# Attention feeding a two-layer network on one core: float64 weights prepared in pairs, with g in pairs of chunks and another issue order

## The chip, the cores and the metric

One core of a Trainium2 chip runs the whole kernel. The metric is the device time of one execution in microseconds (us): for the kernel before, the median of three runs.

## What is computed

The input is q, k, v of shape (8 batches, 8 heads, 576 positions, 64) and f of shape (8, 8, 576), all float32, and two float64 weight matrices of 512 x 2048 and 2048 x 512. Cut to what matters:

```python
scores = q @ k.T / 8;  cum = cumsum(log(clip(f, 1e-4, 1)))
scores = where(causal, -1e9, scores + cum[:, None] - cum[None, :])
attn = softmax(scores);  x = (attn @ v) laid out as (4608 tokens, 512)
h = x @ w_in;  g = h * cos(h);  out = g @ w_out
```

## The kernel before, in words

**Tiling.** The work is 32 pairs of heads (8 batches of 4 pairs) and 16 units of the network (each batch in a unit of 320 tokens and one of 256). A pair's scores come in five row blocks for each of two heads; VectorE masks them and takes the row bound (lines 705, 879), ScalarE takes the exp (715, 884), and the weights of the attention go to f16 high and low parts (901, 905) or, for the first four pairs, stay in float32 (`attention32`). Their product with v, scaled and split into f16 parts xh and xl, is the input of the first layer.

A unit's first layer (`gemm1`, line 964) is four chunks of 512 hidden columns, each four groups of 12 matmuls. A chunk's h is evicted (970), and g = h cos h is made by VectorE and ScalarE (979 to 985) and split into a high and a low f16 part (992, 993 or 994). The second layer (`gemm2`, line 1010) is four blocks of output rows; each reads all four chunks of g, 48 matmuls. So TensorE runs 3072 dense matmuls in either layer.

**The weights.** Each matrix is cut into 16 pieces of 128 rows x 512 columns of 8-byte words, 512 KB. `stage` loads a piece into a raw tile (line 493) and rebuilds float32 from the two halves of each word in three VectorE operations (483, 487, 491) straight into the place of the next piece of W1s or W2s; `bound` squares it on ScalarE with a sum per row (502), as a bound of its size. When all pieces of a group are bounded, the scale follows, and `split` makes the f16 high and low parts in place (512, 519). W1's raw tiles are in the ring "h" (three tiles of 5 KB per partition), which the network's h uses later; W2's are in the ring "g" (eight tiles of 5 KB), which the chunks of g use later. A raw tile is free once its `bound` has run, since that writes its last 256 words as scratch.

**The order.** Every operation is numbered as the program makes it. `ORDER` (line 52) is a list, written out by hand, of all the numbers: `Plan.order` checks it against the dependencies and the ring sizes, and the operations are issued in it (line 1075). Each engine and SyncE's queue run their own operations in this order, each as soon as what it needs is there. A number with "a" runs its alternative on GpSimd (or VectorE). A number with "+n" has n filler matmuls ahead of it:

```python
for pads, fill, fn in seq:
    for _ in range(pads):
        T.matmul(fill(), ones, mask[:, 0:PAD], start=True, stop=True)   # line 1077
    fn()
```

A filler has 448 columns and its result is overwritten. All loads and stores but four go through SyncE's queue, in order; a transfer that waits holds up those behind it. The four are the cumulative rows of the first pair, which ScalarE issues (line 640).

**The opening.** f is loaded (451), clipped (452), its logarithm taken (453) and summed by a scan (455). Rows of that sum go into the tile Q beside q and k (load32: q and k at line 636, the rows at 640); with them the first scores of pair 0 can run (line 697 is the matmul of the pairs 0 to 3, 865 that of pairs 4 to 7, 867 and 868 that of the rest). The probabilities are transposed (668) and evicted (656), multiplied with v (742), and the result transposed again (765). `prep_vscale` loads v once more for a bound of its size (582, 584).

Of the kernel before, what the change touches and what calls it, by code (L numbers as in the profile page):

```python
# [23 lines left out]
P = 128  # L24
# [13 lines left out]
RAWS = {1: "h", 2: "g"}  # L38
CH = {1: 1, 2: 2}
# [9 lines left out]
BUFS = dict(xs=1, stage=2, v2=2, vv=2, pt3=3, pt2=2, xh0=8, xl0=8, xh1=8, xl1=8, h=3, r=1, g=8, ot=1,  # L49
# [11 lines left out]
260 325 544 294 296 545a 238 261 305 256 226 447 314 287a 546 263+1 257 8 326 262 242 239 264a 265 445 393 240 547 319 335 362 266+1 230 297  # L61
288 268 320 298 109 241 322 114 221 301 315 394 302 267 327 321 303 329 227 381 299 548 395 358 549 306 333 289 386 328 359 334 307 345 371
# [259 lines left out]
def fox_moe_kernel(ctx: ExitStack, tc: tile.TileContext, qkT, vp, fT, w1, w2, out):  # L322
# [142 lines left out]

    raws = {}

    def stage(w, k, src, pr):

        n = 1024 if wide else 512  # L470
        rb = ring("raw", [P, n + 256], I32, tag=RAWS[w])
# [4 lines left out]
        def wf():  # L476
            return wide_of(w, k)
# [472 lines left out]
    def gemm1(u, c, pr):  # L950
# [38 lines left out]
        def gx(i):  # L989
            return g.get()[:, i, :, 0:w_]  # L990
# [117 lines left out]
```

## Time and profile before

| | |
|---|---|
| three runs | 1041.29 us median, 1040.98 to 1046.04 |
| profiled execution | 1040.97 us, its span 1039.0 us |
| TensorE matmul, busy | 1027.0 us (99%) |
| TensorE weight loads, busy | 831.6 us (80%) |
| ScalarE, busy | 789.5 us (76%) |
| VectorE, busy | 774.9 us (75%) |
| GpSimd, busy | 294.8 us (28%) |
| DMA | 144.77 MB, mean 139 GB/s |

A row of a group of instructions gives the line, the engine, the operation, what it writes and reads by the program's names, the shape, the count, then the busy time in us and the mean of one in ns, and last the idle time of that engine just before them with what ended it. PE is TensorE's matmuls, PEld its weight loads, DVE VectorE, ACT ScalarE, POOL GpSimd, SP SyncE; SPq is an issue on SyncE's queue. Ends of matmuls are modelled and matmuls overlap, so their starts say more than their durations. The span is the profiled execution's time from the first to the last instruction; the execution's own time is 2 us longer.

### The profile page before, as it was taken

To read this page: it belongs to the slowest core of one execution; us is meant where nothing else is said; L and a number is where in the kernel's file an instruction comes from. 1 tells how busy PE (TensorE), PEld (TensorE's weight loads), DVE (VectorE), ACT (ScalarE), POOL (GpSimd) and SP (SyncE) were. 2 spreads that over 40 slices of the span, in tenths; PEclk is the share of its full clock that TensorE was granted. 3 is DMA by queue.
4 is the path that set the end of the run, shared out by engine and by line. 5 is a ranking of instruction groups with operands and counts; after the bars stand their busy time and mean duration, and the time that the engine had idled before them with its cause. 6 is when DMAs were issued, how large, how long until landed. Compare 5 with 4: busy or idle time off the path is not lost. (4 is left out here: it accounts for less than half of the span.)

```text
span 1039.0 us, 23384 instructions
## 1 busy us (share of the span) xinstructions
PE 1027.0 (99%) x8915; PEld 831.6 (80%) x8916; DVE 774.9 (75%) x1710; ACT 789.5 (76%) x1711; POOL 294.8 (28%) x381
## 2 busy tenths in 40 slices
PE   8999999999999999999999999999999999999998
PEld 4788777778888877888778877888778877888787
DVE  8999998778678676787877688586877967663531
ACT  5999999788768797898877789686878877753431
POOL 3223213432341343332332424233141313300110
PEclk9999999999999999999999999999999999999999
DMA  8997525856685757668465766947466583520001
GB/s 261 288 321 200 130 55 128 185 107 162 154 175 147 163 132 163 139 144 183 114 145 135 176 142 159 193 83 164 124 170 136 121 189 56 122 39 16 7 14 34
DMA packets 255920, 144.77 MB, mean 139 GB/s; under 512 B 223736, under 2 KB 231928, under 8 KB 255808
## 3 DMA queue, kind: packets, MB, share of 16 engines
q1 hardware_dynamic: 255680, 143.27, 58.4%
q8 instruction: 70, 1.15, 0.4%
q14 instruction: 42, 0.34, 0.1%
q10 hardware_dynamic: 128, 0.01, 0.0%
HBM read 71.41 MB, written 9.68 MB: 78 GB/s over the span
## 5 line engine op out<-in xcount | busy, mean ns | idle before, releaser
L1010 PE MATMUL hp<-g,W2s 128*128 128x320 f16 (+1 forms) x3072 | 391.8, 286 | 0.2
L964 PE MATMUL hp<-xh,W1s 128*128 128x320 f16 (+1 forms) x2048 | 381.3, 286 | 1.5 <-ACT h L970 1.4
L964 PEld LDWEIGHTS <-W1s 128*128 128x128 f16 x3072 | 295.5, 98 | 78.6 <-issue 1.8
L1010 PEld LDWEIGHTS <-W2s 128*128 128x128 f16 x3072 | 296.3, 98 | 76.1 <-issue 0.6
L964 PE MATMUL hp<-xl,W1s 128*128 128x256 f16 (+1 forms) x1024 | 292.6, 286 | 0.0
L905 DVE SCALAR_TENSOR_TENSOR PS<-pa,ri,PS 128x576 f16<-128x576 f32 (+3 forms) x280 | 146.1, 544 | 57.3 <-ACT PS L901 55.9
L884 ACT ACTIVATE pa<-pa,nb 128x576 f32<-128x576 f32 (+4 forms) x280 | 141.5, 506 | 48.5 <-DVE nb L879 43.1
L901 ACT ACTIVATE PS<-pa,ri 128x576 f16<-128x576 f32 (+3 forms) x280 | 137.7, 531 | 31.1 <-DVE ri L892 27.0
L889 POOL TENSOR_SCALAR ri<-L 128x1 f32<-128x1 f32 (+1 forms) x168 | 53.9, 321 | 352.0 <-ACT pa L884 347.1
L879 DVE CUSTOM_DVE_ANT_0 pa<-pa,mask 128x576 f32<-128x576 f32 (+4 forms) x280 | 134.7, 500 | 24.0 <-PE pa L868 20.4
L970 ACT ACTIVATE h<-hp 128x320 f32<-128x320 f32 (+1 forms) x256 | 100.1, 411 | 36.5 <-PE hp L964 32.8
L994 POOL TENSOR_TENSOR g<-h,g 128x1024 f16<-128x1024 f32 (+1 forms) x32 | 83.5, 2609 | 149.0 <-ACT g L992 147.3
L985 DVE TENSOR_TENSOR h<-h,r 128x1280 f32<-128x1280 f32 (+1 forms) x64 | 89.6, 1399 | 34.4 <-ACT r L983 33.9
L983 ACT ACTIVATE r<-r,halfpi,m_inv 128x1280 f32<-128x1280 f32 (+1 forms) x64 | 86.2, 1348 | 31.2 <-DVE r L981 29.0
L981 DVE SCALAR_TENSOR_TENSOR r<-r,m_b,h 128x1280 f32<-128x1280 int32 (+1 forms) x64 | 93.6, 1462 | 1.1
L867 PE MATMUL pa<-Q 128*128 128x288 f32 (+4 forms) x288 | 90.4, 327 | 1.2 <-DVE PS L905 0.7
L979 DVE TENSOR_SCALAR r<-h,m_a 128x1280 int32<-128x1280 f32 (+1 forms) x64 | 54.9, 858 | 44.9 <-ACT h L970 43.0
L992 ACT CAST g<-h 128x1280 f16<-128x1280 f32 (+1 forms) x64 | 73.8, 1154 | 10.6 <-DVE h L985 10.4
L934 PEld LDWEIGHTS <-vv 128*64 128x64 f16 x1512 | 68.6, 110 | 10.3 <-issue 9.5
L868 PE MATMUL pa<-Q 68*128 68x288 f32 (+4 forms) x288 | 76.6, 304 | 0.0
L934 PE MATMUL pa<-pt,vv 128*64 128x256 f16 (+2 forms) x1512 | 76.6, 254 | 0.0
L1016 ACT ACTIVATE ot<-hp,m_o 128x320 f32<-128x320 f32 (+1 forms) x64 | 32.2, 503 | 47.6 <-PE hp L1010 36.2
(127 smaller groups left out, 1182.5 us busy)
## 6 DMA issues: line engine op xcount, KB each, us to landing
stage<-in_dram SPq DMA_DIRECT2D x48, 576.0 KB
stage<-in_dram SPq DMA_DIRECT2D x32, 320.0 KB
v<-in_dram SPq DMA_DIRECT2D x32, 320.0 KB
h<-in_dram SPq DMA_DIRECT2D x16, 512.0 KB
g<-in_dram SPq DMA_DIRECT2D x16, 512.0 KB
Q<-Q SPq DMA_DIRECT2D x48, 144.0 KB
out_dram<-ot SPq DMA_DIRECT2D x32, 160.0 KB
Q<-in_dram SPq DMA_DIRECT2D x16, 288.0 KB
```

Source lines behind the costliest of these rows:

```text
L867: T.matmul(c, hi[:, 0, isl], hi[:, 1, d], start=True, stop=False)
L879: op("DVE", c_dve(w) + 0.008, lambda view=view, ib=ib, o=o, w=w, mk=mk, c=c: V.tensor_tensor_reduce(out=view(ib, o, w), in0=view(ib, o, w) ...
L884: op("ACT", c_act(w, True, 2), lambda view=view, ib=ib, o=o, w=w, c=c: A.activation(view(ib, o, w), view(ib, o, w), AF.Exp, bias=nb.get()[ ...
L901: op("ACT", c_act(w, True, 1), lambda view=view, ib=ib, o=o, w=w, c=c, out_=out_: A.activation(out_(0), view(ib, o, w), AF.Copy, scale=ri. ...
L905: op("DVE", c_dve(w) + 0.06, lambda view=view, ib=ib, o=o, w=w, c=c, out_=out_: V.scalar_tensor_tensor(out_(1), view(ib, o, w), ri.get()[: ...
L934: T.matmul(d, vv.get()[:, jb, hd, kv], m, start=first and x == 0, stop=last and x == 2)
L964: T.matmul(hp.get()[:, 0:w_], WS_[1][:, at(1, 4 * c + cb), w, fs], x.get(), start=(n == 0), stop=(n == 11))
L970: op("ACT", c_act(w_, True), lambda hp=hp, k=k: A.activation(h.get()[:, k, 0:w_], hp.get()[:, 0:w_], AF.Copy, scale=float(2.0 ** -24)), re ...
L981: op("DVE", c_dve(N) + 0.045, lambda: V.scalar_tensor_tensor(fl(r), fl(r).bitcast(I32), b1.get()[:, c:c + 1], fl(h), op0=ALU.mult, op1=ALU ...
L983: op("ACT", c_act(N, aps=2), lambda: A.activation(fl(r), fl(r), AF.Sin, scale=inv.get()[:, c:c + 1], bias=halfpi), reads=[inv], writes=[r] ...
L985: op("DVE", c_dve(N), lambda: V.tensor_tensor(fl(h), fl(h), fl(r), op=ALU.mult), reads=[r], writes=hk, prio=pr)
L1010: T.matmul(po.get()[:, 0:w_], WS_[2][:, at(2, 4 * c + k), w, msl], gh.get()[:, i, k, 0:w_], start=(n == 0), stop=(n == 47))
```

## The change

**Pairs.** `stage` and `bound` get a count m of pieces. The first four pieces of W1 (one group) stay single; the other twelve of W1 and all sixteen of W2 are loaded, converted and bounded two at a time, with 1024 words per partition and instruction: 18 loads instead of 32, 54 conversions on VectorE instead of 96, 18 bounds on ScalarE instead of 32. A pair is two rows of 4 KB per partition in the source, as two pieces were. The maxima run over half as many columns. `split` stays as it is.

**Rings.** Raw tiles of pairs, of W1 and W2 alike, are in the ring "g", now four tiles of 10 KB; single ones are in "h". The temporary `chl` of `decay` goes from "g" to "h". Two chunks of g share a tile of 10 KB, so that the ring still holds the g of two units.

**Order.** The program makes 4229 operations instead of 4299, and `ORDER` is another list throughout. Of the 821 groups of matmuls none is added or left out. The fillers:

- before: 99 in 32 places, 44 of them ahead of the first scores (`33+44`). 88 stand ahead of the first group of the first dense layer, and 11 between that and the first group of the second layer.
- after: 119 in 41 places, 52 of them ahead of the first scores (`33+52`). 104 stand ahead of the first group of the first dense layer, 13 between that and the first group of the second layer, 2 later.

The opening of SyncE's queue, by what is moved:

- before: f; W1 pieces 0, 2, 1; Q of pair 0, second head, then first head; W1 piece 3 (waits for the bound of piece 0); v of pair 1 for its bound; a row of pair 1 (waits for the scan); W2 pieces 0 and 1; a row; W1 pieces 4, 5; ...
- after: v of pair 1 for its bound; f; W1 pieces 0, 1, 2; two rows of pair 1 (wait for the scan); Q of pair 0, first head; two rows of pair 1; W1 piece 3 (waits for the bound of piece 0); Q of pair 0, second head; W2 pieces 0 and 1 as a pair; v of pair 0 for its bound; W1 pieces 4 and 5 as a pair; Q of pair 1, both heads; ...

ScalarE's four row copies for pair 0 stand right behind the logarithm before; after, the load of the exp's table stands between.

The core of the diff:

```diff
 RAWS = {1: "h", 2: "g"}
+SOLO = 4
...
-BUFS = dict(..., h=3, r=1, g=8, ot=1,
+BUFS = dict(..., h=3, r=1, g=4, ot=1,
...
-0 50 60 55 70 25 1 2 4 51 27 52 26 72 61 71 53 62 54 63 3 65 11 56 192 57 95 64 100 6 58 125 7a 170 33+44 28 34 35 40+1 66 37 29 36 67 12
...
-        chl = ring("chl", [B * H, 2, S], F32R, tag="g")
+        chl = ring("chl", [B * H, 2, S], F32R, tag="h")
...
-    def stage(w, k, src, pr):
-        n = 1024 if wide else 512
-        rb = ring("raw", [P, n + 256], I32, tag=RAWS[w])
+    def stage(w, k, src, pr, m=1):
+        n = 512 * m * (2 if wide else 1)
+        rb = ring("raw", [P, n + 256 * m], I32, tag=RAWS[m])
...
-        op("SP", T_DGE, lambda: dma(raw()[:, 0:n], src.bitcast(I32)), writes=[rb], prio=pr, size=4 * P * n, ...)
+        op("SP", T_DGE, lambda: dma(raw()[:, 0:n].rearrange("p (a c) -> p a c", a=m), src.bitcast(I32)), writes=[rb], ...)
         if wide:
             for f, fast in ((f1, True), (f2, False), (f3, False)):
-                op("DVE", c_dve(512, fast), f, reads=[rb], writes=wb, prio=pr)
+                op("DVE", c_dve(512 * m, fast), f, reads=[rb], writes=wb, prio=pr)
...
-        op("ACT", c_act(512, aps=1), lambda: A.activation(rb.get()[:, -256:].bitcast(BF16), wide_of(w, k), AF.Square, accum_out=am),
-           reads=[WB[w, at(w, k) + 1].part(j) for j in range(2)], writes=[ab, rb], prio=pr)
+        op("ACT", c_act(512 * m, aps=1), lambda: A.activation(rb.get()[:, -256 * m:].bitcast(BF16), wide_of(w, k, m), AF.Square, accum_out=am),
+           reads=f32_of(w, k, m), writes=[ab, rb], prio=pr)
...
+    def f32_of(w, k, m):
+        return [WB[w, at(w, k) + 1 + i].part(j) for i in range(m) for j in range(2)]
+    def wide_of(w, k, m=1):
+        a = at(w, k) + 1
+        return WS_[w][:, a:a + m].rearrange("p n a c -> p (n a c)").bitcast(F32)
...
-        for i in range(4):
-            stage(1, 4 * c + i, w1v[:, i, c * 512:c * 512 + 512], pr)
-            bound(1, 4 * c + i, ma[:, 4 * c + i:4 * c + i + 1], ab.part(i), pr)
+        st = 1 if 4 * c < SOLO else 2
+        for i in range(0, 4, st):
+            stage(1, 4 * c + i, w1v[:, i:i + st, c * 512:c * 512 + 512], pr, st)
+            bound(1, 4 * c + i, ma[:, 4 * c + i // st:4 * c + i // st + 1], ab.part(i), pr, st)
...
-            stage(2, i, w2v[:, i, :], pr + i / 16)
-            bound(2, i, am[:, i:i + 1], AB.part(i), pr + i / 16)
+            if i % 2 == 0:
+                stage(2, i, w2v[:, i:i + 2, :], pr + i / 16, 2)
+                bound(2, i, am[:, i // 2:i // 2 + 1], AB.part(i), pr + i / 16, 2)
...
-        g = ring("g", [P, 2, 4, UM], F16)
-        gh, gl = g.part(0), g.part(1)
+        if c % 2 == 0:
+            G2[u] = ring("g", [P, 2, 2, 4, UM], F16)
+        g, c2 = G2[u], c % 2
+        gh, gl = g.part((c2, 0)), g.part((c2, 1))
...
-                        T.matmul(po.get()[:, 0:w_], WS_[2][:, at(2, 4 * c + k), w, msl], gh.get()[:, i, k, 0:w_], ...)
+                        T.matmul(po.get()[:, 0:w_], WS_[2][:, at(2, 4 * c + k), w, msl], gh.get()[:, c % 2, i, k, 0:w_], ...)
```

## Rows read from the trace of the kernel before

**Rows 1.** The page: its first line, the busy time of each engine with its share of the span and its instructions, and from part 5 the row of the second layer's high-part matmuls (busy time, mean ns of one, idle time of the engine just before them).

```profile
span 1039.0 us, 23384 instructions
...
PE 1027.0 (99%) x8915; PEld 831.6 (80%) x8916; DVE 774.9 (75%) x1710; ACT 789.5 (76%) x1711; POOL 294.8 (28%) x381
...
L1010 PE MATMUL hp<-g,W2s 128*128 128x320 f16 (+1 forms) x3072 | 391.8, 286 | 0.2
```

**Rows 2.** Busy time of each engine (with its instructions) in five stages, the granted TensorE clock, the busy share of the DMA engines and what they moved. The borders are the first useful matmul, the first dense matmul and two round numbers.

```profile
0.00:12.69 12.69, 10.39 (x44) 5.02 (x45) 9.80 (x17) 4.79 (x8) 6.11 (x24) 1.00 0.74 221
12.69:97.00 84.31, 81.19 (x548) 66.53 (x548) 81.10 (x235) 75.06 (x221) 23.02 (x47) 1.00 0.94 279
97.00:200.00 103.00, 102.23 (x815) 77.55 (x815) 93.97 (x212) 96.46 (x205) 25.34 (x42) 1.00 0.54 124
200.00:1000.00 800.00, 797.61 (x7212) 653.15 (x7210) 578.04 (x1238) 603.04 (x1266) 237.40 (x269) 1.00 0.58 131
1000.00:1039.00 39.00, 35.59 (x303) 29.36 (x300) 11.96 (x11) 10.15 (x14) 2.94 (x1) 1.00 0.07 23
```

**Rows 3.** The chain of waits in order of time, three of its pieces: start, duration, engine, line and matmuls.

```profile
849.74 11.11 PE hp L964 x84
...
903.41 13.21 PE hp L964 x120
...
1001.59 34.01 PE hp L1010 x288
```

**Rows 4.** The same stages for the fillers of line 1077 alone (TensorE's matmuls and weight loads).

```profile
0.00:12.69 12.69, 10.39 (x44) 4.84 (x44) 1.00 0.74 221
12.69:97.00 84.31, 12.25 (x45) 4.47 (x44) 1.00 0.94 279
97.00:200.00 103.00, 3.39 (x11) 1.07 (x11) 1.00 0.54 124
200.00:1000.00 800.00, 0.00 (x0) 0.00 (x0) 1.00 0.58 131
```

**Rows 5.** TensorE's timeline of the first 110 us, five of its pieces: start, duration, and in brackets idle time before it.

```profile
2.29 10.56 PE L1077 MATMUL pa<-mask,ones 128*128 128x448 bf16 x44 [2.29 <-POOL ones L346]
12.69 2.11 PE L697 MATMUL pa<-Q 66*128 66x448 f32 x8
...
32.01 1.68 PE L1077 MATMUL hp<-mask,ones 128*128 128x448 bf16 x8
33.52 0.60 PE L668 MATMUL hp<-eyef,PS 128*128 128x128 f32 x4
...
96.65 0.43 PE L964 MATMUL hp<-xh,W1s 128*128 128x320 f16 x2
```

**Rows 6.** Groups of instructions with the shapes kept apart: VectorE's conversion of W1 pieces (lines 483, 487, 491) and the two forms of line 981. Columns: busy time, mean ns of one, idle time before them.

```profile
L981 DVE SCALAR_TENSOR_TENSOR r<-r,m_b,h 128x1280 f32<-128x1280 int32 x32 | 51.1, 1597 | 0.5
...
L981 DVE SCALAR_TENSOR_TENSOR r<-r,m_b,h 128x1024 f32<-128x1024 int32 x32 | 42.5, 1328 | 0.6
...
L487 DVE SCALAR_TENSOR_TENSOR W1s<-h,W1s 128x512 int32<-128x512 int32 x16 | 10.9, 687 | 0.1
...
L491 DVE SCALAR_TENSOR_TENSOR W1s<-h,W1s 128x512 int32<-128x512 int32 x16 | 10.8, 683 | 0.0
...
L483 DVE TENSOR_SCALAR W1s<-h 128x512 int32<-128x512 int32 x16 | 6.7, 421 | 0.7 <-DMA h<-in_dram 0.3
```

**Rows 7.** The same view for ScalarE: the accumulator read and two forms of the exp (line 884), and the bound of a W1 piece (line 502).

```profile
L884 ACT ACTIVATION_READ_ACCUMULATOR pa<-pa,nb 128x1 f32 x280 | 57.6, 206 | 0.0
...
L884 ACT ACTIVATE pa<-pa,nb 128x576 f32<-128x576 f32 x56 | 40.1, 716 | 16.1 <-DVE nb L879 14.9 <-DVE ri L892 0.8
...
L884 ACT ACTIVATE pa<-pa,nb 128x448 f32<-128x448 f32 x56 | 34.2, 611 | 13.0 <-DVE nb L879 11.4 <-DVE ri L892 1.0
...
L502 ACT ACTIVATE h<-W1s 128x512 bf16<-128x512 f32 x16 | 10.2, 640 | 4.0 <-DVE W1s L491 4.0
```

**Rows 8.** TensorE's groups by line between 12.7 and 200 us, those with idle time of 0.2 us or more that work of another engine or a load ended (last columns).

```profile
L964 PE MATMUL hp<-xh,W1s 128*128 128x320 f16 (+1 forms) x256 | 47.8, 286 | 0.4 <-ACT h L970 0.3
...
L697 PE MATMUL pa<-Q 66*128 66x288 f32 (+4 forms) x96 | 26.6, 401 | 1.6 <-DMA Q<-in_dram 0.7 <-ACT PS L715 0.6 <-issue 0.3
L865 PE MATMUL pa<-Q 66*128 66x288 f32 (+4 forms) x96 | 26.2, 399 | 0.3 <-DVE ri L892 0.3
L668 PE MATMUL hp<-eyef,PS 128*128 128x128 f32 x120 | 17.6, 275 | 1.1 <-ACT PS L715 1.1
...
L765 PE MATMUL hp<-eyef,xs 128*128 128x128 f32 x20 | 3.6, 280 | 0.2 <-DVE m_w L443 0.2
```

**Rows 9.** The issues of the weight loads on SyncE's queue (line 493): duration of the issue, least, median and most, in ns, and first and last start.

```profile
L493 SPq DMA_DIRECT2D h<-in_dram x16: 328/336/564, 1.4 to 58.5; - x16
...
L493 SPq DMA_DIRECT2D g<-in_dram x16: 327/424/1558, 12.0 to 101.8; - x16
```

**Rows 10.** SyncE's timeline, its first piece: the issue of the load of f.

```profile
0.79 0.60 SPq L451 DMA_DIRECT2D vv<-in_dram  x1
```

**Rows 11.** VectorE's timeline: the clip of f and the scan.

```profile
3.72 0.82 DVE L452 TENSOR_SCALAR vv<-vv 64x576 f32<-64x576 f32 x1 [0.29 <-DMA vv<-in_dram]
5.30 1.35 DVE L455 TENSOR_TENSOR_SCAN vv<-vv 64x576 f32<-64x576 f32 x1 [0.75 <-ACT vv L453]
```

**Rows 12.** What SyncE's queue waited for, the row of the W1 loads: us in total, times, longest.

```profile
SPq L493 <- ACT h L502: 19.8, 10, 5.2
```

More of the change, by code (lines that the diff above doesn't have):

```diff
@@ L466, in fox_moe_kernel @@
     raws = {}
-    def stage(w, k, src, pr):
-        n = 1024 if wide else 512
-        rb = ring("raw", [P, n + 256], I32, tag=RAWS[w])
+    def stage(w, k, src, pr, m=1):
+        n = 512 * m * (2 if wide else 1)
+        rb = ring("raw", [P, n + 256 * m], I32, tag=RAWS[m])
         raw = rb.get
         raws[w, k] = rb
-        wb = [WB[w, at(w, k) + 1].part(j) for j in range(2)]
+        wb = f32_of(w, k, m)
         def wf():
-            return wide_of(w, k)
+            return wide_of(w, k, m)
         def word(which):
@@ L526, in prep_w1 @@
         ab = Buf()
-        for i in range(4):
-            stage(1, 4 * c + i, w1v[:, i, c * 512:c * 512 + 512], pr)
-            bound(1, 4 * c + i, ma[:, 4 * c + i:4 * c + i + 1], ab.part(i), pr)
+        st = 1 if 4 * c < SOLO else 2
+        for i in range(0, 4, st):
+            stage(1, 4 * c + i, w1v[:, i:i + st, c * 512:c * 512 + 512], pr, st)
+            bound(1, 4 * c + i, ma[:, 4 * c + i // st:4 * c + i // st + 1], ab.part(i), pr, st)
         yield
-        op("DVE", 0.07, lambda: V.tensor_reduce(m1.get(), ma[:, 4 * c:4 * c + 4], axis=AX.X, op=ALU.max),
-           reads=[ab.part(i) for i in range(4)], writes=[m1], prio=pr)
+        op("DVE", 0.07, lambda: V.tensor_reduce(m1.get(), ma[:, 4 * c:4 * c + 4 // st], axis=AX.X, op=ALU.max),
+           reads=[ab.part(i) for i in range(0, 4, st)], writes=[m1], prio=pr)
         clamp(m1, pr)
@@ L553, in f1 @@
             for c in range(4):
-                V.tensor_reduce(m[:, c:c + 1], am[:, 4 * c:4 * c + 4], axis=AX.X, op=ALU.max)
-        op("DVE", 0.28, f1, reads=[AB.part(i) for i in range(NF)], writes=[MB], prio=p2)
+                V.tensor_reduce(m[:, c:c + 1], am[:, 2 * c:2 * c + 2], axis=AX.X, op=ALU.max)
+        op("DVE", 0.28, f1, reads=[AB.part(i) for i in range(0, NF, 2)], writes=[MB], prio=p2)
         op("POOL", 0.2, lambda: G.tensor_scalar(m, m, float(2.0 ** -80), float(2.0 ** 126), op0=ALU.max, op1=ALU.min), writes=[MB], prio=p2)
@@ L946, in attention @@
                 yield
-    GT = {}
+    GT, G2 = {}, {}
     def gemm1(u, c, pr):
@@ L1009, in mm @@
                     for w, i in ((0, 0), (1, 0), (0, 1)):
-                        T.matmul(po.get()[:, 0:w_], WS_[2][:, at(2, 4 * c + k), w, msl], gh.get()[:, i, k, 0:w_], start=(n == 0), stop=(n == 47))
+                        T.matmul(po.get()[:, 0:w_], WS_[2][:, at(2, 4 * c + k), w, msl], gh.get()[:, c % 2, i, k, 0:w_], start=(n == 0), stop=(n == 47))
                         n += 1
```

280 lines of the change are left out of this document (148 added, 132 removed), and 25 rows, old and new, of the table ORDER.

## The prediction

> **What bounds the kernel now.** I read the page first, then the stages, then TensorE's timeline, then what the other engines spend on the weights. The page's busy line [rows 1] shows TensorE busy for 1027.0 of 1039.0 us and VectorE and ScalarE for three quarters. The stages [rows 2] show where the missing 12 us lie: 2.3 us before the first filler matmul, 3.1 us from 12.69 to 97 us (no dense layer yet), 0.8 us from 97 to 200, 2.4 us in the 800 us after that, and 3.4 us at the end, when the last output is evicted and stored. VectorE is 96% busy from 12.69 to 97 us (81.10 of 84.31) and ScalarE 94% from 97 to 200, but after 200 us both are near 75%. So even where VectorE is full, TensorE waits little.
>
> A busy matmul engine could still run slack, because matmuls overlap in the record. What decides is the spacing of starts [rows 3]: 120 matmuls of 256 columns take 13.21 us, 110 ns each, deep in the body, and 84 of 320 columns take 11.11 us, 132 ns each. The whole closing run, where no other engine feeds TensorE much, has 288 matmuls in 34.01 us, 118 ns each, between these two. The dense matmuls run at the same spacing in the middle as at the end: TensorE is the bound, and its instruction stream, in program order, is nearly the time.
>
> That stream holds fillers: the matmuls of line 1077, written into ORDER as "+n". They take TensorE's time like any other. Their stage table [rows 4] has 44 before 12.69 us, 45 up to 97 us, 11 after, none after 200 us (one straddles a border). In the opening [rows 5] the first useful matmul starts at 12.69 us, right behind the 44th filler, with no wait in its row: the fillers, not the data, set that moment. Eight fillers in a row start at 32.01 us and the next work at 33.52: 0.189 us for one.
>
> **The change part by part.** *Matmuls.* No matmul of the reference is added, removed or resized; only the index into g changes. Cost nothing, and no gain: 6144 dense matmuls and all of the attention stay.
>
> *Fillers.* ORDER has 99 of them before and 119 after. The first group grows from 44 to 52: 8 x 0.189 = +1.5 us before the first useful matmul. The other groups grow from 55 to 67: 12 x 0.189 = +2.3 us, most of it ahead of the first matmul of the first dense layer (44 became 52). A filler is free only where TensorE would have waited anyway; but the waits of before are outside the fillers already [rows 2], so a longer list can be paid back only from the 3.1 + 0.8 + 2.4 = 6.3 us of visible waiting. Sum so far: +3.8 us.
>
> *Conversion in pairs.* 14 pairs replace 28 single pieces (four stay single). VectorE: a piece costs 421 + 687 + 683 ns [rows 6]. The trace has no such instruction of 1024 words. Bounds: twice the single (no saving), or the slope of line 981, (1597 - 1328) / 256 = 1.05 ns per element, which leaves 687 - 538 = 149 ns that is paid once per instruction. I take the slope, since line 981 is the same kind of operation; it saves 14 x 3 x 0.149 = 6.3 us of VectorE, or 0 at the other bound. For the bound on ScalarE the slope of line 884, (716 - 611) / 128 = 0.82 ns, leaves 640 - 420 = 220 ns, and the accumulator read of 206 ns falls away once per pair [rows 7]: 14 x 0.43 = 6.0 us. Both lie beside TensorE. What reaches the end is only what shortens a wait of TensorE for these engines. From 12.7 to 200 us those waits are [rows 8] 0.6 (line 697 for the exp), 1.1 (668), 0.3 (865), 0.3 (964) and 0.2 (765): 2.5 us. Between nothing and all of it I take half, -1.25 us: the savings fall in that stretch, but the new order rearranges who waits for whom.
>
> *Loads in pairs.* The same bytes in 18 transfers instead of 32, each with the same 4 KB runs; SyncE issues 14 fewer, of 0.34 us (W1) or 0.42 (W2) by the medians [rows 9]. The DMA engines are 94% busy from 12.69 to 97 us at 279 GB/s [rows 2], and TensorE waited for a load 0.7 us in all [rows 8], so faster or slower issue is worth from -0.7 to, if a pair lands later than its first half did, +1.9 us (524,288 B at 279 GB/s) at one place; I take 0.
>
> *The opening of SyncE's queue.* A v piece now goes ahead of f, and the load of Q for the first head stands behind two copies of cumulative rows that wait for the scan; behind it wait Q's second head and the first pair of W2. Before, f was issued at 0.79 us and used at 3.72 [rows 10, 11]. Now 0.6 us of issue and 327,680 B at 221 to 279 GB/s [rows 2], 1.2 to 1.5 us, go ahead: the scan, which ended at 6.65 us, ends near 8.5. Two row copies of some 0.6 us follow, then Q: issued by 10.3. Its 294,912 B take 1.0 to 1.3 us, and f showed 2.3 us from issue to use including 0.5 to 0.7 of transfer, so Q is there near 13.2. The fillers now end at 12.69 + 1.5 = 14.2: 1.0 us of cover, cost 0. If the estimate is short by 2.5 us, TensorE waits 1.5.
>
> *Ring of four and g in pairs.* A weight pair's slot returns after both halves are converted and bounded: by the slopes 0.69 + 2 x 1.22 + 1.26 = 4.4 us after work on it begins, against 1.79 + 0.84 = 2.6 for a single piece: 1.8 us later. In the dense layers a g pair returns when the last matmuls have read its second half, 12 matmuls or 1.3 to 1.6 us after the first. TensorE waited 0.2 us for anything on line 1010 [rows 1], since g is two units deep before and after; cost 0, bounded by 1.6 us per reuse if that cover is gone.
>
> **Sum.** The profiled execution took 1040.97 us: +1.5 + 2.3 - 1.25 = **1043.5 us**. It lies 0.3 us under the median of 1041.29, so I leave the sum there.
>
> A rule of the Trainium skill speaks the other way. Perfetto Trace Analysis, section Identifying the Most-Contended Engine, says that matmul busy time is no good measure of headroom and that the busy share of the weight loads is one. Here that share is 80% [rows 1], which would leave room for the 6 us saved on each of the other engines to show. The spacing of the matmul starts [rows 3] disagrees.
>
> **The rivals.** *Slower: the queue behind the ring.* SyncE issues in order and already waited 19.8 us in 10 places for the bound of a W1 piece [rows 12]. Ten of the 14 pairs must wait for a slot; each wait is up to 1.8 us longer, and loads of Q and v for the next head pair stand behind it. It decides if that happens ahead of the first dense matmul (97 us), where TensorE has nothing else but fillers: three such places are 5.4 us, and with nothing recovered 1040.97 + 3.8 + 5.4 = 1050.2. Against it: only 0.7 us of waiting for loads before, and fewer issues. Chance 0.20.
>
> *All waits recovered.* If the visible 6.3 us vanish, 1040.97 + 3.8 - 6.3 = 1038.5. For it: VectorE at 96% in the opening loses 6 us of work there. Against: 2.4 of the 6.3 us lie after 200 us, where no weights are handled. Chance 0.15.
>
> *TensorE was not the bound.* Then the larger saving, 6.3 us, and the waits of the opening count together: at 0 for the fillers, 1040.97 - 6.3 = 1034.7. Only the skill's rule speaks for it, nothing in the rows. Chance 0.05.
>
> *The change doesn't save anything.* If an instruction of twice the length costs twice, nothing is recovered: 1044.8. It belongs to the forecast's case.
>
> **How the numbers follow.** The forecast's case, 1041 to 1047, has 0.60. A measurement tells 0.5% from no change, 5.2 us: 1036.1 to 1046.5. Faster: the last real rival alone, 0.05. Same: recovered waits 0.15 and 0.55 of the forecast. Slower: 0.20 and the top 0.05 of the forecast. The range runs from 1038.5 (all recovered) to 1048.5: it holds the forecast's case, most of the recovered one, and the lower half of the slower one, whose price may come in one or two places instead of three; about 0.15 is left out.
>
> **What would show it.** In the profile after: the first useful matmul at about 14.2 us; 119 fillers, still 0.189 us apart; the first dense matmul of line 964 about 3 us later than 96.65; dense matmuls still 110 and 132 ns apart; conversions of 1024 words near 0.69, 1.22 and 1.22 us; TensorE's idle time after 14 us between 4 and 7 us. Wrong would be: a first matmul that waits for Q behind its fillers, waits of several us of TensorE for Q or v before 100 us (the slower rival), idle time near zero (the recovered one), or a changed spacing.

## The result, and the profile after

The kernel after takes 1050.83 us (median of 9 runs, 1049.42 to 1054.33) against 1042.49 for the kernel before in the same comparison (9 runs, 1039.64 to 1048.66): a ratio of 1.0077, 95% interval 1.0049 to 1.0104. It is slower by 0.8%. The forecast was 1043.5, with a range up to 1048.5 and most weight on no change beyond 0.5%: the time lies above that range. The profiled execution after took 1049.58 us with a span of 1047.9; against [rows 1] that is 8.9 us more span.

The page after answers to [rows 1]:

```profile
span 1047.9 us, 23329 instructions
...
PE 1030.1 (98%) x8936; PEld 833.5 (80%) x8936; DVE 770.2 (74%) x1653; ACT 790.7 (75%) x1683; POOL 341.3 (33%) x411
...
L1017 PE MATMUL hp<-g,W2s 128*128 128x256 f16 (+1 forms) x3072 | 393.0, 286 | 0.6 <-DVE g L1000 0.3
```

TensorE's busy time grew by 3.1 us; the rest of the 8.9 is waiting. GpSimd has 46.5 us more work: the new ORDER sends 138 instead of 118 operations to it. The stages, cut as in [rows 2], and the fillers alone (now line 1084), as in [rows 4]:

```profile
0.00:13.89 13.89, 11.60 (x53) 5.69 (x53) 9.37 (x16) 4.89 (x8) 5.13 (x23) 1.00 0.60 187
13.89:97.00 83.11, 77.86 (x522) 63.47 (x521) 77.03 (x192) 70.27 (x193) 30.29 (x46) 1.00 0.88 283
97.00:200.00 103.00, 101.76 (x819) 77.64 (x819) 92.76 (x198) 97.93 (x194) 40.29 (x49) 1.00 0.56 120
200.00:1000.00 800.00, 794.34 (x7175) 650.22 (x7175) 577.30 (x1238) 605.40 (x1270) 262.46 (x292) 1.00 0.59 131
```

```profile
0.00:13.89 13.89, 11.60 (x52) 5.50 (x52) 1.00 0.60 187
13.89:97.00 83.11, 14.42 (x53) 5.39 (x52) 1.00 0.88 283
97.00:200.00 103.00, 4.42 (x13) 1.32 (x13) 1.00 0.56 120
```

Up to 97 us TensorE stands idle for 83.11 - 77.86 = 5.3 us behind its first useful matmul, where it was 3.1. From 200 to 1000 us it is 5.7 instead of 2.4. VectorE, 96% busy in the opening before, is now at 93%; over the whole run its busy time fell by 4.7 us, and ScalarE's rose by 1.2 although its bounds took 5.8 less. TensorE's timeline, its pieces that answer to [rows 5] and two new waits:

```profile
2.29 11.76 PE L1084 MATMUL pa<-mask,ones 128*128 128x448 bf16 x52 [2.29 <-POOL ones L345]
13.89 1.08 PE L702 MATMUL pa<-Q 66*128 66x448 f32 x4
...
19.04 1.10 PE L702 MATMUL pa<-Q 66*128 66x320 f32 x4 [1.09 <-DMA Q<-in_dram]
...
46.09 0.22 PE L440 MATMUL hp<-dg,ones 128*128 128x128 bf16 x1 [1.36 <-POOL dg L437]
...
101.54 0.44 PE L969 MATMUL hp<-xh,W1s 128*128 128x320 f16 x2
```

The dense layers begin 4.9 us later than before, where the forecast had 3. TensorE's waits in the whole run, costliest first (us in total, times, longest); the 0.6 and 1.1 us of [rows 8] for line 715's exp are gone, and others have come (line 1084 waits for its first operand before and after):

```profile
PE pa L872 <- DVE PS L910: 4.3, 7, 1.1
PE pa L1084 <- POOL ones L345: 2.3, 1, 2.3
PE hp L440 <- POOL dg L437: 1.4, 1, 1.4
PE pa L702 <- DMA Q<-in_dram: 1.1, 1, 1.1
PE hp L1084 <- ACT h L975: 1.0, 1, 1.0
```

The pairs' own durations came out as forecast. Conversions and bound of W1 in pairs, to be read beside [rows 6, 7]; one run of dense matmuls for [rows 3], still 110 ns apart; and what SyncE's queue waited for to load a pair, for [rows 12]:

```profile
L486 DVE SCALAR_TENSOR_TENSOR W1s<-g,W1s 128x1024 int32<-128x1024 int32 x6 | 7.3, 1218 | 0.0
L490 DVE SCALAR_TENSOR_TENSOR W1s<-g,W1s 128x1024 int32<-128x1024 int32 x6 | 7.3, 1217 | 0.0
L482 DVE TENSOR_SCALAR W1s<-g 128x1024 int32<-128x1024 int32 x6 | 4.1, 680 | 0.5 <-DMA g<-in_dram 0.5
L501 ACT ACTIVATE g<-W1s 128x1024 bf16<-128x1024 f32 x6 | 6.4, 1068 | 0.0
```

```profile
912.37 13.20 PE hp L969 x120
```

```profile
SPq L492 <- ACT g L501: 6.3, 4, 3.4
```

**Where the 1.36 us come from.** TensorE's matmul of line 440 waits for dg, a small diagonal tile that GpSimd makes on the way to a chunk's scale. GpSimd's and VectorE's timelines around it:

```profile
42.63 1.28 POOL L408 TENSOR_SCALAR m_w<-m_w 128x1 f32<-128x1 f32 x1 [0.97 <-PE hp L673]
44.01 2.03 POOL L437 TENSOR_SCALAR dg<-eye,m_w 128x128 bf16<-128x128 bf16 x1
```

```profile
42.60 1.22 DVE L486 SCALAR_TENSOR_TENSOR W1s<-g,W1s 128x1024 int32<-128x1024 int32 x1
43.74 0.75 DVE L522 SCALAR_TENSOR_TENSOR W1s<-W1s,s 128x512 f16<-128x512 f32 x1
44.40 1.23 DVE L490 SCALAR_TENSOR_TENSOR W1s<-g,W1s 128x1024 int32<-128x1024 int32 x1
```

A clamp of 128 numbers takes 1.28 us and ends at 43.91, 0.08 us behind the conversion that was running (42.60 + 1.22 = 43.82). dg begins inside line 522, and line 490 begins before it is through: it ends 0.41 us behind that one. In the first 110 us, 12 of GpSimd's small instructions take 0.5 us or more and end 0.05 to 0.10 us (three dg: 0.41 to 0.50) behind a two-input VectorE instruction that ran meanwhile; left alone they take about 0.2 (dg 0.63). Two more end so behind line 482, which has one input. GpSimd is held while VectorE runs such an instruction. That is not new: in the kernel before, 14 of its small instructions in the first 110 us took over 0.1 us more than their usual length, 5.6 us in all, and after it is again 14, but 10.3 us. The change made the two-input conversions 1.22 us long. It also moved two more dg of W1 to GpSimd: before and after,

```profile
L438 POOL TENSOR_SCALAR dg<-eye,m_w 128x128 bf16<-128x128 bf16 x2 | 1.8, 906 | 0.2
```

```profile
L437 POOL TENSOR_SCALAR dg<-eye,m_w 128x128 bf16<-128x128 bf16 x4 | 5.6, 1390 | 0.4
```

The Trainium skill says this (SBUF — State Buffer, section SBUF: two separate sides): VectorE and GpSimd share a pair of ports, and a VectorE instruction with two inputs in SBUF (beside a GpSimd one that reads SBUF), or a GpSimd one, holds it for its whole length while the other stands. These rows agree; for line 482 the page would need a two-port mode. That its second 512 words cost 0.26 us (0.416 single, 0.680 in a pair) where line 486's cost 0.53 (0.690, 1.218) fits one and doesn't prove it. VectorE is held behind GpSimd too, in the body, where the longest of TensorE's 4.3 us of waits (1.1 at 390.7 us) follows from it:

```profile
385.94 3.84 DVE L986 SCALAR_TENSOR_TENSOR r<-r,m_b,h 128x1280 f32<-128x1280 int32 x1
389.70 0.81 DVE L910 SCALAR_TENSOR_TENSOR PS<-pa,ri,PS 128x576 f16<-128x576 f32 x1
```

```profile
385.82 2.61 POOL L1001 TENSOR_TENSOR g<-h,g 128x1280 f16<-128x1280 f32 x1 [1.28 <-ACT g L999]
```

Line 986 takes 1.60 us [rows 6]; behind GpSimd's 2.61 it takes 3.84, and line 910 and TensorE wait.

### The profile page after: what moved, and what is told of

It is laid out like the page before. It is cut to its first block, busy times and chain, and to the rows that moved or that the text cites. A ratio compares the mean times of both kernels' runs of the same rounds, so it can differ in the third digit from the quotient of the medians.

```text
span 1047.9 us, 23329 instructions
## 1 busy us (share of the span) xinstructions
PE 1030.1 (98%) x8936; PEld 833.5 (80%) x8936; DVE 770.2 (74%) x1653; ACT 790.7 (75%) x1683; POOL 341.3 (33%) x411
## 4 chain that ended last, share of the span: by engine, by line
PE 80%; ACT 7%; DVE 5%; DMA 3%; issue 2%; POOL 1%; ACTq 0%; SPq 0%; POOLq 0%; DVEq 0%
PE hp L1017 33%; PE hp L969 30%; PE pa L939 6%; PE pa L872 4%; PE pa L873 3%; PE pa L870 1%; ACT pa L889 1%; DMA g<-in_dram 1%; PE hp L747 1%; DMA pt<-PS 1%; ACT PS L906 1%; DVE pa L884 1%; PE pa L702 1%; DVE r L986 1%; ACT r L988 1%
## 5 line engine op out<-in xcount | busy, mean ns | idle before, releaser
L1017 PE MATMUL hp<-g,W2s 128*128 128x256 f16 (+1 forms) x3072 | 393.0, 286 | 0.6 <-DVE g L1000 0.3
L969 PE MATMUL hp<-xh,W1s 128*128 128x256 f16 (+1 forms) x2048 | 381.4, 286 | 0.2 <-ACT h L975 0.2
L1001 POOL TENSOR_TENSOR g<-h,g 128x1024 f16<-128x1024 f32 (+1 forms) x32 | 89.1, 2785 | 140.2 <-ACT g L999 139.8
L990 DVE TENSOR_TENSOR h<-h,r 128x1280 f32<-128x1280 f32 (+1 forms) x64 | 93.8, 1466 | 34.2 <-ACT r L988 33.9
L999 ACT CAST g<-h 128x1280 f16<-128x1280 f32 (+1 forms) x64 | 73.8, 1155 | 10.3 <-DVE h L990 9.0
L807 POOL CAST Q<-stage 128x1152 fp32r<-128x1152 f32 x33 | 41.4, 1255 | 104.9 <-PE pa L872 74.0
```

Source lines behind the costliest of these rows:

```text
L969: T.matmul(hp.get()[:, 0:w_], WS_[1][:, at(1, 4 * c + cb), w, fs], x.get(), start=(n == 0), stop=(n == 11))
L1017: T.matmul(po.get()[:, 0:w_], WS_[2][:, at(2, 4 * c + k), w, msl], gh.get()[:, c % 2, i, k, 0:w_], start=(n == 0), stop=(n == 47))
```

## The experiments

Every run was compared with the kernel before on the same chip. The table holds what their traces say, worked out from TensorE's records: when ScalarE first evicts the first unit's hidden layer ("first h", us), the sum of TensorE's idle time from 14 us to it and behind it, and the lowest granted clock of the stretches 14 to 40, 40 to 70 and 70 to 100 us.

| run | first h | idle to it | idle behind | clock | median us | ratio (95%) |
|---|---|---|---|---|---|---|
| before | 99.5 | 3.1 | 3.2 | 1.00 | 1042.49 | |
| after | 105.0 | 5.3 | 6.9 | 1.00 | 1050.83 | 1.0077 (1.0049, 1.0104) |
| e1 | 117.5 | 7.7 | 8.6 | 0.61 | 1065.41 | 1.0213 (1.0189, 1.0238) |
| e2 | 132.7 | 11.0 | 7.6 | 0.66 | 1082.90 | 1.0394 (1.0351, 1.0437) |
| e3 | 105.1 | 4.9 | 5.5 | 1.00 | 1049.17 | 1.0066 (1.0048, 1.0084) |
| e4 | 116.7 | 7.6 | 10.6 | 0.59 | 1069.34 | 1.0266 (1.0245, 1.0288) |
| e5 | 101.7 | 5.7 | 8.0 | 1.00 | 1050.66 | 1.0080 (1.0045, 1.0114) |
| e6 | 102.8 | 3.4 | 7.4 | 1.00 | 1048.51 | 1.0043 (1.0026, 1.0061) |
| e7 | 111.2 | 8.8 | 8.1 | 0.77 | 1054.90 | 1.0101 (1.0067, 1.0134) |
| e8 | 108.5 | 5.9 | 7.5 | 0.87 | 1053.78 | 1.0089 (1.0054, 1.0123) |
| e9 | 101.1 | 1.8 | 4.0 | 1.00 | 1044.08 | 1.0016 (1.0003, 1.0029) |
| e10 | 103.6 | 3.6 | 6.1 | 1.00 | 1047.88 | 1.0050 (1.0033, 1.0068) |
| e11 | 102.3 | 3.8 | 4.9 | 1.00 | 1045.90 | 1.0040 (1.0021, 1.0059) |
| e12 | 113.2 | 6.1 | 8.5 | 0.82 | 1058.58 | 1.0144 (1.0119, 1.0169) |
| e13 | 103.7 | 3.9 | 7.2 | 1.00 | 1049.61 | 1.0087 (1.0070, 1.0104) |
| e14 | 104.1 | 4.2 | 7.1 | 1.00 | 1049.12 | 1.0074 (1.0059, 1.0089) |
| e15 | 109.6 | 5.1 | 7.6 | 0.80 | 1051.97 | 1.0107 (1.0088, 1.0125) |
| e16 | 106.1 | 6.2 | 4.3 | 0.93 | 1048.66 | 1.0073 (1.0051, 1.0094) |
| e17 | 102.4 | 2.0 | 7.3 | 1.00 | 1048.44 | 1.0031 (1.0007, 1.0056) |
| e18 | 101.8 | 2.2 | 7.4 | 1.00 | 1048.27 | 1.0033 (1.0012, 1.0055) |

Each row is one profiled execution, so chance is in it. Where two runs share an opening (after and e3, e1 and e4, e6 and e10), first h agrees within 0.9 us and the idle time to it within 0.4. A run can stray further. The kernel after, e3 and e17 are the same program up to the matmul of line 702 that starts at 42.64 us in the kernel after, and yet e17 is there 1.3 us sooner; the kernel after and e17:

```profile
42.64 1.08 PE L702 MATMUL pa<-Q 66*128 66x448 f32 x4
```

```profile
41.37 1.08 PE L702 MATMUL pa<-Q 66*128 66x448 f32 x4
```

The difference arises in the first 30 us. The ten runs that begin like the kernel after (52 first fillers, the same order of loads) start their first useful matmul between 13.83 and 14.76 us. The wait of 1.09 us for Q at 19.04 is in the kernel after alone. A wait near 28 us, ahead of the second pair's first scores, which nothing in the profile releases ("issue"), is 0.49 us in the kernel after, 1.42 in e3, 1.90 in e15 and none in e17:

```profile
28.14 1.16 PE L702 MATMUL pa<-Q 66*128 66x448 f32 x4 [0.49 <-issue]
...
28.50 1.16 PE L701 MATMUL pa<-Q 66*128 66x448 f32 x4 [1.42 <-issue]
...
28.77 1.30 PE L711 MATMUL pa<-Q 66*128 66x448 f32 x4 [1.90 <-issue]
...
26.87 1.16 PE L702 MATMUL pa<-Q 66*128 66x448 f32 x4
```

What an edit does later is better read from that matmul of line 702 on (us; the idle time is TensorE's on that way):

| run | it starts | from it to first h | idle on the way |
|---|---|---|---|
| after | 42.64 | 62.36 | 2.76 |
| e3, same opening as after | 42.76 | 62.34 | 2.68 |
| e8, Q first | 46.13 | 62.37 | 2.77 |
| e13, halved loads | 41.30 | 62.37 | 2.77 |
| e14, halved conversions | 42.15 | 61.93 | 2.45 |
| e15, halved bounds | 46.91 | 62.68 | 2.84 |
| e6, all halved | 41.37 | 61.40 | 2.05 |
| e10, same opening as e6 | 41.64 | 62.01 | 2.46 |
| e17, three dg on VectorE | 41.37 | 61.04 | 1.09 |
| e18, e17 with halved loads | 40.72 | 61.04 | 1.08 |

e6 and e10, alike so far, differ by 0.6 us: a step of that size isn't told apart here, one of 1.3 us that comes twice is. The times, with intervals of 2 to 5 us, tell less.

**The pairs or the list? (e1, e2)**

```
e1: program after; ORDER = before's list in after's numbers, a pair at its second piece's place
e2: program before; ORDER = after's list in before's numbers
```

> The program after (pairs, ring of four, g in pairs) issued in the list of before, translated number by number: a pair's load and conversions stand where the second of its two single pieces stood; 11 of 4229 operations come somewhat earlier because the ring of four needs it (largest: one bound, 149 places). 99 fillers as before. Theory A (the loss is the new list: its 20 more fillers and the waits that it makes, nothing in the pairs): like before within 0.3%, some 1039 to 1043 us, TensorE's idle time in its rows near 8.6 us in all. Theory B (the pairs make it: VectorE instructions of 1.2 us, the ring of four, g in pairs): like after, 1047 to 1052 us, with waits of TensorE for VectorE or ScalarE of 13 us or more in all.

> The program before (single pieces, rings h of three and g of eight) issued in the list of after, each pair replaced by its two pieces one behind the other; 12 operations come earlier and some loads later because the ring h of three needs it. 119 fillers as after. Theory A: as slow as after or a little slower, since 6 us of savings on VectorE are gone too: 1049 to 1055 us. Theory B: like before plus at most the fillers, 1041 to 1045 us.

Each half without the other is far slower than the two together. In e1 TensorE waits 4.1 us for VectorE's dg at 77.6 us, and the granted clock behind it lies between the two levels, 1.2 and 2.4 GHz:

```profile
PE hp L439 <- DVE dg L432: 4.1, 1, 4.1
```

```profile
70.00:100.00 30.00, 25.59 (x114) 22.83 (x113) 16.14 (x43) 17.29 (x47) 2.00 (x7) 0.61 0.54 158
```

A list fits one set of durations; neither the pairs nor the list can be priced by exchanging the other in the opening.

**Opening or body? (e3, e4)**

```
e3: ORDER = after's list up to unit 2's first layer (near 205 us), then before's
e4: the reverse (e1's opening, after's body)
```

> The program after; its own list up to the first matmul of unit 2's first layer (near 205 us), and from there the list of before, translated. 117 fillers. If the loss of 8.6 us is half in the opening (first dense matmul 4.9 us late in the profile after) and half in the body's waits, this gives before + 4.5 to 5.5: 1045 to 1048 us, with idle time of TensorE after 200 us near 2.4 us. If the body's waits come from the pairs of g or the shared tiles, they stay: 1049 to 1051 us.

> The other half: the program after, the list of before, translated, up to the first matmul of unit 2's first layer, then the list of after. 101 fillers. Theory A: before + 3 to 4.5, 1044 to 1047 us: first dense matmul near 96.7 us as before, idle time of TensorE after 200 us near 5.7 us. Theory B: as after, with a late first dense matmul.

The waits of line 872 for line 910 (4.3 us) go with the new list's body and come back in e4 (4.2). They belong to the list and not to the pairs, for e2, with single pieces, has them too (its lines 867 and 905):

```profile
PE pa L867 <- DVE PS L905: 4.3, 7, 1.1
```

In e3 the idle time behind first h is 1.4 us less and the profiled span 1.4 us less (1046.4), with two fillers fewer; in the median it can't be told from the kernel after.

**W2 in pairs alone, in before's list (e5, e12, e16)**

```
e5:  stage(2, i, ..., 2) and ring g=4 as after; W1 in single pieces; 99 fillers; ORDER of before
e12: e5, each pair's load, conversions and bound issued as two of one piece
e16: e5, with the pair at its first piece's place in ORDER instead of the second's
```

> W2's eight pairs and g in pairs of chunks (ring g of four tiles of 10 KB), W1's pieces single in the ring h as before, issued in the list of before: only one bound comes 40 places earlier and five matmul groups of the last units some 20. 99 fillers. Theory A (the list makes the loss, not the pairs): like before within 0.4%, 1038 to 1045 us, no stall of TensorE over 1 us between 60 and 100 us. Theory B (long instructions and g in pairs make it): over half of the loss, 1046 us and more. Theory C (the ring of four that W1 and W2 share makes the loss, which forced another list): like A here, since W1 keeps its own ring, while the same list stalled and fell to half the clock at 70 to 100 us when both shared it.

> The kernel before, its list and its 99 fillers, with W2 and g in rings of four pair tiles, as in the run that came out at 1.008, but each pair's load, three conversions and bound issued as two instructions of one piece. Only the grain of the rings and of the list's places is then left of the pairing. If the length of the instructions cost those 8 us, it comes back to 1042.5 to 1044 (ratio under 1.002) and the eviction of unit 1's hidden layer from 143.8 to about 137 us. If it is that both pieces of a pair now stand at one place of the list, and that a tile comes free and is loaded two pieces at a time, it stays over 1.005. Half and half: 1046.

> As the run of W2 and g in pair rings in the list of before (1.008; 1.0144 with halves), but each pair's load, conversions and bound stand at the place of its first piece in the list, not of its second. If what cost 8 us there was that half of the pieces were loaded and converted later than listed (the last load landed at 83.0 us, VectorE stood 1.6 us for it, and TensorE lost 2.9 us of 30 behind it), the eviction of unit 1's hidden layer comes at 137 us or before and the ratio falls to 1.003 or less. If it is the pair as such (both pieces' work in one place of an in-order queue), it stays at 1.006 or more, with the waits moved to earlier softmax blocks.

Without one filler more, half of the pairing costs the same 8 us. In e5 a pair load issued at 66.96 us is used at 83.01, and VectorE's queue stands for it (SyncE's and VectorE's timelines):

```profile
66.96 0.44 SPq L492 DMA_DIRECT2D g<-in_dram  x1
```

```profile
83.01 0.69 DVE L482 TENSOR_SCALAR W2s<-g 128x1024 int32<-128x1024 int32 x1 [1.63 <-DMA g<-in_dram]
```

Issuing the pieces one by one at the same place made it worse (e12); moving the pair forward moved the loss. Against the kernel before, TensorE's matmuls fall behind by 8.7 us between 35 and 150 us in e5 and by 1.7 in e16; but e16 loses 3.8 us between 29 and 36 us, with one wait there and a granted clock of 0.93 from 14 to 40 us:

```profile
32.76 1.10 PE L702 MATMUL pa<-Q 66*128 66x320 f32 x4 [2.39 <-issue]
```

My guess in e16 that the place was at fault holds where the loss of e5 lay, and is refuted for the time. That two pieces' work and transfer stand at one place of an in-order queue is what is left as the cost; it is argued, not shown.

**Fillers and Q (e7, e8, e9, e11)**

```
e7:  after, only the first group of 52 (the other 67 dropped)
e8:  after, first group 44; SyncE begins f, W1, Q, Q, v as before
e9:  before, 119 fillers (52 first, twelve later places +1)
e11: e10 with a first group of 44
```

> The program and list after with the first 52 fillers alone; the other 67 are left out. If they only stand where TensorE would wait anyway, the time stays: 1049 to 1052 us, their 12.5 us turned into waits in its rows. If they are in the way, as the prediction took them, up to 12.5 us faster: 1038 us and up. If the waits without fillers make the clock fall, slower than after, with a granted clock under 1.00 in the first 100 us.

> The program and list after with 44 instead of 52 first fillers and the head of SyncE's queue as before: f, the first three pieces of W1, Q of both first heads, then v. If the late opening (first useful matmul 1.2 us later, 1.1 us of waiting for the second head's Q at 19 us) goes through to the end: after - 1.5 to 2.6, 1047.5 to 1049.5 us. If later waits are set by VectorE and ScalarE instead, the gain is gone by the first dense matmul (still near 101.5 us) and the time is as after.

> The kernel before with 119 fillers instead of 99: 52 instead of 44 in the first group, and one more in twelve of the later places. Nothing else is changed. If each filler is paid in full, as the forecast had it (20 x 0.189 us), 1046.3 us where the kernel before has 1042.5 (ratio 1.0036), and the first ScalarE eviction of the first unit's hidden layer comes 3.8 us later than 99.5. If the later fillers only stand in waits that TensorE has anyway (the idle time of 3.1 us between 14 us and that eviction shrinks as they grow), the eight of the first group at most are paid: 1042.5 to 1044 (1.000 to 1.0015).

> The run beside it (halves, before's body) with 44 instead of 52 fillers in the first group, the order of the loads untouched. If the first group is paid in full, 1.5 us less than that run. If VectorE and ScalarE set when the opening goes on, the eight turn into idle time of the same size further on (0 to -0.5 us), and if that idle time lowers the granted clock between 14 and 70 us, as it did where the fillers were cut before, 1 to 4 us more.

e9 prices the 20 fillers: 1.7 us by the ratio (0.3 to 3.0), +1.6 us by first h and +2.9 by the profiled span, not 3.8. The idle time to first h falls from 3.1 to 1.8 us: part of the fillers stands in waits. e7 shows the other side: with 67 fillers fewer the median is 4 us above the kernel after's, not 12.7 below (67 x 0.19; the ratios' intervals overlap), at a clock of 0.77:

```profile
40.00:70.00 30.00, 27.36 (x157) 24.50 (x157) 24.20 (x57) 23.00 (x61) 10.29 (x12) 0.77 0.64 224
```

An earlier Q with eight fillers fewer (e8) gained nothing: TensorE then waited 2.3 us for ScalarE's exp in 14 to 40 us. In e11 eight fillers fewer took 2.0 us off e10's median; the two intervals overlap.

**The length of the instructions (e6, e13, e14, e15, e10)**

```
e6:  for j in range(m): each pair's dma, f1, f2, f3 and activation on one 512-column piece
e13: only the dma so;  e14: only f1, f2, f3;  e15: only the activation
e10: e6 with e3's list
```

> The program after in its own list and rings, with each pair's load, three conversions and bound issued as two instructions of one piece each, so that only the length of the instructions is undone. Theory A and C: as slow as after or 0 to 5 us slower, since 6 us of work come back on VectorE and on ScalarE in the opening: 1050 to 1056 us. Theory B: faster than after by 2 us and more.

> The kernel after with only the loads halved: each pair is loaded by two DMA issues of 512 KB (some 0.33 us each on SyncE against 0.40 for the pair), conversions and bounds stay whole. If the 2 us that the halves gave back came from the transfers (the first piece lands before the second, and the small loads behind are served between them), the first eviction of the hidden layer goes from 105.0 to about 103 us and TensorE's idle time between 14 us and it from 5.25 to about 3.4. If they came from the length of the engines' instructions, it stays at 105 (or 105.3 for the longer issue) and 5.2.

> The kernel after with only the three conversions on VectorE halved (0.68 us pieces instead of 1.22 us, 42 instructions more and some 6 us more work on VectorE). If the softmax work that stands behind a conversion in VectorE's queue was what TensorE waited for, the eviction goes from 105.0 to about 103 us and the idle time from 5.25 to about 3.4; if VectorE's busy time decides in place of its grain, the 6 us show and it goes to 107 or more.

> The kernel after with only the bound on ScalarE halved (0.63 us pieces with an accumulator read each instead of 1.07 us). If the evictions and the softmax behind a bound in ScalarE's queue were what TensorE waited for, 105.0 goes to about 103 us and 5.25 to about 3.4; if ScalarE's busy time decides, 107 or more. If each of the three runs gives back under 1 us, the halves' 2 us are a sum of small pieces on several engines.

> The kernel after with both mends at once: every pair's load, conversions and bound issued as two instructions of one piece (as in the run of halves, 1.0043), and from the third unit on the list of before (as in the run with before's body, 1.0066). The rings of four and g in pairs stay, 117 fillers. If the two are parts of one sum, the idle time of TensorE falls to about 11 us (14.45 less 1.4 for the halves, less 1.8 for the body) and the time to 1046.5 us, ratio 1.004 or less; what is left over the kernel before is then 18 fillers (3.4 us) and some 1 us of later Q. If the body's list is worth nothing in time, as its own run left open, it stays at the halves' 1048.5 (1.0055). If the rings or g in pairs hold more, it does not come below 1048.5 either and the idle time behind 205 us stays near 4 us.

With all instructions halved, first h comes 2.2 us earlier, although VectorE and ScalarE get their saved work back; but 1.3 of the 2.2 lie ahead of 42.64 us, where e17, with nothing halved, is as early. Behind it all halves give 1.0 us (0.4 in e10), halved conversions 0.4, halved loads and bounds nothing. The 1.3 us by which e13's first h is early lie wholly ahead of 42.64 us, and e15's low clock (0.80) follows the wait of 1.90 us at 28.77, in the slowest of its four executions (1055.24 against 1050.44 to 1052.76): neither can be put down to the halves. In e14 GpSimd's clamp and dg, the two rows above, read:

```profile
42.21 0.74 POOL L408 TENSOR_SCALAR m_w<-m_w 128x1 f32<-128x1 f32 x1 [0.98 <-PE hp L681]
43.05 0.91 POOL L437 TENSOR_SCALAR dg<-eye,m_w 128x128 bf16<-128x128 bf16 x1
```

Together they take 1.66 us less than in the kernel after, and TensorE's wait of 1.36 us is gone, which e8 and e13, with whole conversions, have to the hundredth; later ones (0.67 us for another dg at 71.11) take most of it back. e10 has 1.3 us less idle time behind first h than e6 and 0.9 less span (1045.7); its time (1.0050 against 1.0043, with overlapping intervals) doesn't show it.

**GpSimd or VectorE's own queue? (e17, e18)**

```
e17: after, ORDER:  247a -> 247   475a -> 475   362a -> 362    (dg on VectorE)
e18: e17 with e13's halved loads
```

> The kernel after with three of the diagonal tiles dg (chunks 1, 3 and 2 of W1) made on VectorE, at the same places of the list, in place of GpSimd; nothing else is changed. In the profile after, GpSimd's instruction for chunk 1's dg runs from 44.01 to 46.04 us, ending behind a VectorE conversion of a pair (44.40 to 45.63), where such a tile takes 0.63 us elsewhere, and TensorE waits 1.36 us for it. If GpSimd is held while a long VectorE instruction with two inputs runs, dg is there by 44.3 us, that wait goes, the first eviction of the hidden layer comes near 104 us instead of 105.0 and the time falls by up to 1 us (ratio near 1.0068). If the 2.0 us are only how such a span is recorded, TensorE waits about as long at the same place (for VectorE's chain in place of GpSimd's) and the eviction stays at 105.

> The same with each pair's load issued as two of one piece; conversions and bounds stay whole. The loads' halves gave 1.3 us by the eviction (103.7), the conversions' halves 0.9 (104.1), all halves 2.2 (102.8). If the conversions' share of that was GpSimd being held off, this run reaches 102.8 to 103 us and 1048.5 us without halving a conversion, ratio near 1.005. If the conversions' share came from VectorE's own queue (softmax work behind a long instruction), it stays at 103.7 and 1049.5.

First h comes 2.6 us earlier and the idle time to it falls from 5.3 to 2.0 us. Half of that isn't the edit's: 1.3 us and 1.6 us of it lie ahead of the matmul at 42.64 us, behind which the first moved dg stands. From there on the three letters are worth 1.3 us by first h and 1.7 us of idle time, in e17 and again in e18. dg and line 440 in e17, then its stages:

```profile
42.67 0.25 DVE L433 TENSOR_SCALAR dg<-eye,m_w 128x128 bf16<-128x128 bf16 x1
```

```profile
43.30 0.22 PE L440 MATMUL hp<-dg,ones 128*128 128x128 bf16 x1
```

```profile
14.00:40.00 26.00, 25.09 (x143) 18.34 (x142) 23.42 (x65) 19.68 (x57) 7.33 (x11) 1.00 1.00 320
40.00:70.00 30.00, 29.59 (x213) 25.05 (x211) 29.76 (x69) 28.17 (x78) 9.30 (x15) 1.00 0.95 324
```

The profiled span falls by 2.4 us to 1045.5, with the 1.3 us of the start in it; the median, 1048.44, is 2.4 under the kernel after's, though the two ratios' intervals overlap. The conversions stay 1.22 us long and stand in VectorE's queue as before, so that queue was not what TensorE waited for; e17 and e14, where a dg left on GpSimd beside shorter conversions no longer makes TensorE wait at line 440's place near 44 us, agree that it was GpSimd being held. That dg takes 0.25 us on VectorE against 0.63 on a free GpSimd may be part of the gain. Halving the loads adds nothing behind that matmul (e18). The effect is near my expectation of 1 us.

## Why the prediction was wrong

**TensorE is the bound**: right. Dense matmuls keep their 110 ns, and fillers and idle time sum up to the loss: 1.2 us for the first group (13.89 against 12.69), 2.3 for twelve later ones at 0.19, and 14.45 - 8.57 = 5.9 us of idle time are 9.4, against 8.9 of span. The rival by which TensorE was not the bound gained nothing, though conversions and bounds took 5.3 and 5.8 us less.

**Fillers**, +3.8: on top of the kernel before they cost 1.7 (e9). The count was right, and so was the first group's end (14.2 forecast, 13.83 to 14.76 in the ten runs above); that they are paid in full was not, and e7 shows that many of them cover waits and keep the clock.

**Conversion in pairs, -1.25**: the step that failed. Its durations held (0.68, 1.22, 1.22 us; VectorE's conversions 5.3 us less by their groups, the bounds 5.8). But I let TensorE's waits only shrink, by half of 2.5 us, with no term for waits that the longer instructions and the new list make. TensorE's idle time behind 14 us rose from 6.3 to 12.2 us, where I had 4 to 7: +5.9 in place of -1.25. What stood there:

- 2.1 of the 5.9 us lie ahead of first h. The longer two-input conversions hold GpSimd, on which the new list put all four dg of W1, so that the scales of W1, their splits and TensorE's matmuls come late. Moving three dg off GpSimd gave back 1.7 us of idle time and 1.3 us by first h (e17, e18). The waits of the first 30 us (1.6 us in the profiled execution) change from execution to execution.
- 3.7 of the 5.9 us lie behind first h. There the new list makes 4.3 us of waits for line 910, with pairs or single pieces (e2). With before's list there (e3) they go and others come: 2.4 of the 3.7 us stay and were not traced.

No line of the prediction looked at GpSimd, whose row [rows 1] showed 28% and no cause for care.

**Loads in pairs**, 0: no run contradicts it behind 42.64 us, where halved loads change nothing (e13, e18). What they do ahead of it can't be told from the chance of one execution. W2's pairs cost 8 us in before's list (e5, e16); how much of that the new list avoids isn't shown.

**Opening of SyncE's queue**, 0: nearly right. The first head's Q was covered; the second head's cost 1.09 us at 19.04 in the profiled execution, and nothing in the nine other runs that begin like it. Putting Q first (e8) did not pay.

**Ring of four, and g in pairs**, 0: right. SyncE waits 6.3 us in 4 places for a pair's bound, less than [rows 12]. So the slower rival, the queue behind the ring at 1050.2, came close in time by luck: what it rests on did not happen.

**The body**, to which the prediction gave no term: the new list brought 3.3 us more idle time from 200 to 1000 us; 4.3 us are waits for line 910. Two of the seven (1.1 and 0.9 us) follow a VectorE instruction held by GpSimd, as shown at 385.94. The others were not traced to a cause.

What stays open: how the 2.9 us by first h that e17 still has over the kernel before divide between fillers (16 of the 20 lie ahead of 97 us; 1.6 us by e9), the pairs and the chance of the start; what sets the wait near 28 us; and why halving and before's body together (e10) stay 0.5% above the kernel before.

## What to carry to other kernels

Making an instruction longer saves its fixed part on its own engine, and lengthens the time for which it stands in everyone else's way: look up who waits in its queue and whom it holds before counting the saving. A list ordered by hand or by a planner fits the durations that it was made for, so a changed duration and a changed list can only be judged together, and best by the wait of the bound engine, place by place. When a small instruction takes several times its usual length, look at what another engine ended just before it. Two profiles are two executions: look first at the last instruction ahead of which both programs are the same, and put to the edit only what differs behind it.

## What the runs showed of the hardware

- GpSimd's small instructions (0.2 us; dg 0.63) took up to 1.3 and 2.0 us beside VectorE's two-input instructions and ended 0.05 to 0.10 us (dg 0.41 to 0.50) behind them; the other way round, VectorE's 1.60 us became 3.84 behind GpSimd's 2.61.
- A conversion of 1024 words costs 1.22 us against 2 x 0.69 for two of 512, the one-input first step 0.68 to 0.72 against 2 x 0.42.
- Behind single waits of TensorE of 4.1 us (e1), 2.3 us (e8) and 1.9 us (e15) in the opening the granted clock of the stretch was 0.61, 0.87 and 0.80, a mix of its two levels, and first h came 12.5, 3.5 and 4.6 us later than in the kernel after: the loss is more than the wait. Not every such wait did it: the kernel after waited 1.36 us at a clock of 1.00.
- The same program reached the same matmul near 42 us at 41.37, 42.64 and 42.76 us in three executions (e17, after, e3).
